# Decode through two attention and GEGLU layers on one core: layer norm in two products, a transpose inside PSUM, the gate's second half in two pieces, and one more V head kept

## The chip, the cores and the metric

The kernel runs on 1 core of a Trainium2 chip, as one launch. The metric is the device time of that core in microseconds (us). The kernel before was timed in three runs: 293.29, 294.82 and 295.31 us, median 294.82. A separate execution was recorded by the hardware profiler; it took 291.89 us, and its instructions span 290.1 us.

## What is computed

Two layers, each attention followed by a feed-forward block, with **the same weights and the same K/V cache in both layers**. There are 4 batches of one token each, width 512, 32 query heads over 8 K/V heads of 128, a cache of 4096 positions, and a feed-forward width of 1792. All inputs are bf16.

```python
def _A_ref(x, k_cache, v_cache, wq, wo):
    q = (x @ wq) ...                                   # 32 heads of 128
    scores = jnp.einsum("bhqd,bhkd->bhqk", q, k) * (Dh ** -0.5)
    p = _softmax(scores, axis=-1)
    o = jnp.einsum("bhqk,bhkd->bhqd", p, v)
    return o ... @ wo

def _B_ref(x, w_gate, w_up, w_down):
    return (_gelu(x @ w_gate) * (x @ w_up)) @ w_down

x = A_x
x = x + _A_ref(_layernorm(x), A_k_cache, A_v_cache, A_wq, A_wo)
x = x + _B_ref(_layernorm(x), B_w_gate, B_w_up, B_w_down)
x = x + _A_ref(_layernorm(x), A_k_cache, A_v_cache, A_wq, A_wo)
x = x + _B_ref(_layernorm(x), B_w_gate, B_w_up, B_w_down)
```

A K or V head of one batch is 4096 x 128 bf16, which is 1 MB. All K and V of the four batches together are 64 MB, the weights are some 13.5 MB.

## The kernel before

**Order of the work.** A small planner (class `Plan`) is given every step with its engine, an estimated duration and its dependencies. It lays the steps out in a list, the one with the longest remaining path first, shifted by the table `LEAD`. The list is then emitted step by step, so each engine runs its own steps strictly in the planned order and waits in place when a step isn't ready. The planner's durations decide order only; they aren't times of the chip. Each step's name appears below in quotes.

**Batches and layers.** The batches go one after the other. Inside batch b the first layer (L = 0) runs whole: scores of all 8 heads ("sc", in two halves z of four heads, each in two parts m), softmax ("mx", "bi", "ex", "pt", "pw", "pc", with the sums "su" and "rc"), values head by head ("val", in two halves m of 16 products), scaling by the softmax sum ("os"), output projection ("op", with the half sums "yo" and "ys"), layer norm, and feed-forward ("up", "ft", "ga" and so on to "dn"). Then follow a layer norm, the query projection of the second layer ("qm", "qe", "qt", "qs", "qp", "qx") and the second layer's scores. The second layer's values of batch b are computed while batch b+1 loads and runs its first layer. The second layer's projection and feed-forward are done once, for all four batches, at the very end.

**Loads.** All large loads are issued by SyncE (SP) in one fixed order, and each load is spread over all 16 DMA engines. K and V go through 12 slots of 1 MB each (`SLOTS`, tile KV). A load waits, on SP, until the last reader of its slot's old contents is done; everything behind it on SP waits too. K of batch b is loaded once and serves both layers. V is loaded once per layer, except for the heads in `HELD[b]`, which keep their slot from the first layer to the second. `HELD` is `((), (7,), (7,), (7,))`: in batch 0 no head is kept. The loads in `HALVES` come as two loads of 512 KB (`ld_part`, L357), the others whole (`ld_head`, L351). After the down-projection weights come the K heads of batch 1: as long as free slots last they are issued early, the others wait for the second layer's first scores of batch 0, step ("sc", 0, 1, 0, 1), which frees four slots.

**Steps named in the prediction.** K heads are transposed on VectorE (DVE) in place, two steps per head ("tn", L366). The layer norm squares x ("lnq", L500), sums x and x² in one fp32 product into R_ps[1] ("lnm", L506), takes both sums with one reduction (L512), subtracts the mean (L513) and computes the variance ("lnv", L521 and L522). The query projection of half z is a product into R_ps[z] (L538), copied to SBUF as bf16 by ScalarE (ACT) ("qe", L551), transposed by DVE (L556), spread with a mask ("qs", L595), replicated by a small product ("qp", L605) and expanded into the scores' weights ("qx", L392). In the feed-forward both products come out with tokens on partitions; "ft" (L662) transposes one of them from PSUM to SBUF on DVE; "ga" (L678 to L681) and an exponential on ACT (L688) make the gelu's argument; L697 and L699 multiply by the norm's factor and by the other half; L705 to L707 finish the gelu and write the bf16 product; L715 is the down projection; L646 and L647 transpose its result and add it to x.

At the end of the kernel the values of batch 3's second layer run in the order of heads 0, 1 to 3, 7, 4 and 5, 6. The projection of all but head 6 goes into R_ps[0] (L613); its two halves are copied by ACT (L632) and summed into R_ps[1] by products (L639), and head 6's own products (L623) are added there. Spare products of the identity (L1004) fill waits on TensorE (PE).

Of the kernel before, what the change touches and what calls it, by code (L numbers as in the profile page):

```python
# [11 lines left out]
ACT = mybir.ActivationFunctionType  # L12
# [9 lines left out]
HELD = ((), (7,), (7,), (7,))  # L22
HALVES = {(b, 1, j) for b in range(3) for j in range(8)} | {(3, 1, 6)}
# [7 lines left out]
DMA_FETCH = 1.5  # L31
DMA_LEAD = 4.0

PATIENCE = (0.5, 1.5, 0.7)
LEAD = {"tn1": -3, "val0": 1, "sc10": -2, "chain": 2, "sc11": -6, "sm00": 1, "os0": -6, "op": -2, "sm01": 11, "sm10": 10, "qx1": 4, "other": 5, "sc00": 2, "sm11": 8, "os1": -4, "tn0": -2, "sc01": 1}
EARLY = {("pt", 1): 60.0, ("su", 1): 60.0}
WINDOW = 3.413
WARM = 0.45
FILL = 0.7
SPIN = 0.22  # L40
STREAM = {"sc": 0.85, "qm": 0.85, "up": 0.75, "up2": 0.75, "kt": 0.21, "pw": 0.16, "qp": 0.11, "qn": 0.05,
          "su": 0.02, "lnm": 0.03, "xt": 0.1, "ys": 0.2, "dn": 0.38, "dn2": 0.38}


def stage(n):
# [13 lines left out]
    if n[0] in ("lnq", "lnm", "lnc", "lnv", "lnr", "up", "ft", "ga", "gb", "gy", "gc", "zz", "dn", "da", "qm", "qe",  # L59
                "qt", "qn", "qc", "qk"):  # L60
        return "chain"
# [3 lines left out]
class Plan:  # L65
# [149 lines left out]
    def warm(self, places):  # L215
# [3 lines left out]
        for n, _ in self.order:  # L219
# [16 lines left out]
            past.append((z, last, 0.72 * d if kind == "val" else d - 0.15 if kind in ("op", "op2") else STREAM.get(kind, 0.0)))  # L236
# [4 lines left out]
def kernel(  # L241
# [22 lines left out]
    FT = F // 4  # L264
    scale = float(Dh) ** -0.5
# [237 lines left out]
    def ln_mm(bs, nb):  # L503
        def emit():
            st = R_ps[1][:, 0:2 * CD * nb].rearrange("p (s k b) -> p s k b", s=2, k=CD)
            nc.tensor.matmul(st, lhsT=ones_mean, rhs=XS[:, :, :, bs], start=True, stop=True)  # L506
        return emit

    def ln_mid(bs, nb):
        def emit():  # L510
            st = R_ps[1][:, 0:2 * CD * nb].rearrange("p (s k b) -> p s b k", s=2, k=CD)
            nc.vector.tensor_reduce(out=mu[:, :, 0:nb], in_=st, axis=AX.X, op=ALU.add)  # L512
# [5 lines left out]
    def ln_var(nb):  # L518
        def emit():
            t = lt[:, 0:nb]  # L520
# [12 lines left out]
    def qmm(z, bs, nb):  # L533
# [7 lines left out]
        return emit  # L541

# [46 lines left out]
    def qsplit(z, b):  # L589
        def emit():  # L590
            if b:
# [17 lines left out]
    def proj(src, nb, heads, first, last):  # L609
        def emit():  # L610
            for j in heads:
                for i in range(4):
                    nc.tensor.matmul(R_ps[0][32 * i:32 * i + nb, :], lhsT=src[:, 4 * j + i, 0:nb],  # L613
# [4 lines left out]
    def proj_last(src, nb, heads, last):  # L618
# [433 lines left out]
```

## Time and profile before

| quantity | value |
| --- | --- |
| median of three runs | 294.82 us (293.29 to 295.31) |
| profiled execution | 291.89 us, span of its instructions 290.1 us |
| HBM read | 111.42 MB, 384 GB/s over the span |
| PE busy | 236.3 us (81%), 67.7 of it the spare products of L1004 |
| DVE busy | 133.5 us (46%) |
| ACT busy | 74.5 us (26%) |
| granted TensorE clock | 0.998 of full speed |

Busy time of an engine says little here: PE fills its waits with products that compute nothing. The rows of use are those of the DMA engines, the chain of waits (which follows the work that ended last back to what released it), and the timeline. In timelines, a row gives the start in us from the span's start, the duration, the engine, the line, the operation and how many instructions were merged; in brackets stands the idle time before it and what ended it.

### The profile page before, as it was taken

Reading aid. Unit: us, or ns where it says so; the run is one execution under the profiler, and the core shown is the slowest. Engines: PE = TensorE matmul, PEld = TensorE weight load, DVE = VectorE, ACT = ScalarE, POOL = GpSimd, SP = SyncE. Lnnn points to the kernel's source line nnn. Section 1 sums busy time; section 2 is a strip of 40 time slices with the busy share of each in tenths; the row PEclk is TensorE's granted clock in tenths of the full one; section 3 lists DMA queues with packets and bytes.
Section 4 is the critical chain, followed back from the end, with each engine's and each line's share of the span. In section 5 each row is a group of like instructions: output and inputs, shape, how many; then the busy total and the mean of one; then the engine's idle time right before and its main releaser. Section 6 shows DMA issues by size and latency. Waiting matters only on the chain.

```text
span 290.1 us, 9733 instructions
## 1 busy us (share of the span) xinstructions
PE 236.3 (81%) x4419; PEld 138.3 (48%) x4419; DVE 133.5 (46%) x380; ACT 74.5 (26%) x167; POOL 0.7 (0%) x6
## 2 busy tenths in 40 slices
PE   4988887878687888798888698879977889897794
PEld 1433454443233565455434465554445655565552
DVE  4149911002289942052389721343998213444034
ACT  1020751001023852101224731000338321113010
POOL 0000000000000000000000000000000000000000
PEclk9999999999999999999999999999999999999999
DMA  7999999999999999999999999999999999999910
GB/s 312 412 421 419 376 405 416 414 371 426 415 407 395 419 421 417 402 407 406 393 417 416 425 416 411 405 407 390 413 422 416 408 387 403 396 382 420 411 47 1
DMA packets 21657, 112.04 MB, mean 386 GB/s; under 512 B 2032, under 2 KB 6128, under 8 KB 12272
## 3 DMA queue, kind: packets, MB, share of 16 engines
q1 hardware_dynamic: 21568, 111.42, 95.3%
q8 instruction: 34, 0.56, 0.8%
q14 instruction: 7, 0.06, 0.0%
q10 hardware_dynamic: 48, 0.01, 0.0%
HBM read 111.42 MB, written 0.00 MB: 384 GB/s over the span
## 4 chain that ended last, share of the span: by engine, by line
DMA 62%; PE 16%; SPq 11%; DVE 7%; issue 2%; ACT 1%; DVEq 0%
DMA KV<-in_A_v_cache_dram 43%; DMA KV<-in_A_k_cache_dram 8%; SPq L351 7%; PE O_ps L485 7%; DMA wd_sb<-in_B_w_down_dram 6%; DMA wq_sb<-in_A_v_cache_dram 5%; SPq L741 3%; PE S_ps L415 3%; DVE KV L366 2%; PE R_ps L715 1%; PE R_ps L538 1%; DVE PA L662 1%; PE S_ps L1004 1%; PE R_ps L655 1%; DVE sm L421 1%
## 5 line engine op out<-in xcount | busy, mean ns | idle before, releaser
L485 PE MATMUL O_ps<-PA,KV 128*128 128x56 bf16 x1920 | 66.3, 188 | 20.8 <-DMA KV<-in_A_v_cache_dram 17.3
L485 PEld LDWEIGHTS <-KV 128*128 128x128 bf16 x1920 | 57.6, 97 | 40.8 <-DMA KV<-in_A_v_cache_dram 32.4
L1004 PE MATMUL S_ps<-iden_b 128*128 128x512 bf16 x226 | 67.7, 401 | 3.6 <-DVE iden_b L321 3.6
L366 DVE STREAM_TRANSPOSE KV<-KV 128x1024 int32<-128x1024 int32 x48 | 56.5, 1214 | 0.6 <-DMA KV<-in_A_k_cache_dram 0.4
L379 ACT ACTIVATE KV<-R_ps 128x512 bf16<-128x512 f32 x64 | 34.9, 595 | 28.0 <-PE R_ps L373 27.9
L415 PE MATMUL S_ps<-KV,PA 128*32 128x512 bf16 x384 | 35.3, 394 | 2.1 <-DVE KV L366 1.3
L1004 PEld LDWEIGHTS <-iden_b 128*128 128x128 bf16 x227 | 21.9, 107 | 27.6 <-issue 11.7
L373 PE MATMUL R_ps<-iden_b,KV 128*128 128x128 bf16 x256 | 22.1, 219 | 6.3 <-ACT KV L379 3.1
L421 DVE TENSOR_REDUCE sm<-S_ps 128x1 f32<-128x512 f32 x16 | 10.8, 677 | 27.4 <-PE S_ps L415 27.4
L373 PEld LDWEIGHTS <-KV 128*128 128x128 bf16 x256 | 15.8, 97 | 14.8 <-issue 10.2
L415 PEld LDWEIGHTS <-PA 128*32 128x32 bf16 x384 | 11.4, 94 | 13.2 <-issue 4.4
L493 DVE TENSOR_TENSOR OT<-O_ps,XS 128x4 bf16<-128x4 f32 (+1 forms) x12 | 2.0, 164 | 32.9 <-PE O_ps L485 32.9
L415 PE MATMUL S_ps<-KV,QN 128*32 128x512 bf16 x128 | 16.8, 381 | 0.2 <-ACT KV L379 0.2
L438 ACT ACTIVATE PA<-S_ps,sm 128x512 bf16<-128x512 f32 x16 | 11.7, 732 | 20.4 <-DVE sm L432 17.6
L632 ACT ACTIVATE PA<-R_ps 128x256 f32<-128x256 f32 x10 | 3.8, 384 | 46.2 <-PE R_ps L613 41.1
L529 ACT ACTIVATE sm<-sm 128x1 f32<-128x1 f32 (+1 forms) x10 | 2.0, 203 | 52.6 <-DVE sm L522 52.6
L493 DVE TENSOR_TENSOR OT<-O_ps,rdk 128x16 bf16<-128x16 f32 (+3 forms) x18 | 3.1, 170 | 26.7 <-PE O_ps L485 26.7
L463 ACT ACTIVATE PA<-T_ps 128x512 bf16<-128x512 f32 x16 | 9.6, 597 | 13.0 <-PE T_ps L455 11.8
L556 DVE STREAM_TRANSPOSE PA<-PA 128x256 int32<-128x256 int32 x10 | 4.4, 437 | 14.9 <-ACT PA L551 14.2
L613 PE MATMUL R_ps<-wo_sb,OT 128*1 128x512 bf16 (+1 forms) x124 | 8.7, 378 | 2.6 <-DMA wo_sb<-in_A_wo_dram 1.4
L646 DVE STREAM_TRANSPOSE PA<-R_ps 128x128 f32<-128x128 f32 x9 | 2.9, 317 | 16.5 <-PE R_ps L623 10.2
L447 DVE STREAM_TRANSPOSE PA<-PA 128x256 int32<-128x256 int32 x16 | 7.0, 434 | 7.5 <-ACT PA L438 7.5
(92 smaller groups left out, 173.9 us busy)
## 6 DMA issues: line engine op xcount, KB each, us to landing
KV<-in_A_v_cache_dram SPq DMA_DIRECT2D x34, 1024.0 KB, 15.0
KV<-in_A_k_cache_dram SPq DMA_DIRECT2D x32, 1024.0 KB, 13.5
KV<-in_A_v_cache_dram SPq DMA_DIRECT2D x46, 512.0 KB, 7.0
wq_sb<-in_A_wq_dram SPq DMA_DIRECT2D x1, 4096.0 KB, 12.2
wo_sb<-in_A_wo_dram SPq DMA_DIRECT2D x2, 2048.0 KB, 19.5
wq_sb<-in_A_v_cache_dram SPq DMA_DIRECT2D x4, 1024.0 KB
wg_sb<-in_B_w_gate_dram SPq DMA_DIRECT2D x1, 1792.0 KB
wu_sb<-in_B_w_up_dram SPq DMA_DIRECT2D x1, 1792.0 KB
```

The costliest lines, as they stand in the source:

```text
L351: nc.sync.dma_start(out=where[name], in_=src.rearrange("(p c) d -> p (c d)", p=P))
L366: nc.vector.transpose(out=w, in_=w)
L373: nc.tensor.matmul(R_ps[k % 2][:, P * u:P * u + P], lhsT=where[name][:, at:at + P], rhs=iden_b[:], start=True, stop=True)
L379: nc.scalar.activation(out=where[name][:, 512 * k:512 * k + 512], in_=R_ps[k % 2][:], func=ACT.Copy)
L415: nc.tensor.matmul(S_ps[z][32 * t:32 * t + 32], lhsT=w, rhs=k, start=(m == 0 and x == 0), stop=(m == 1 and x == 3))
L421: nc.vector.tensor_reduce(out=cms[:, z:z + 1], in_=S_ps[z][:].rearrange("p c r -> p (c r)"), axis=AX.X, op=ALU.max)
L438: nc.scalar.activation(out=PW[L][z].rearrange("p (a r e) -> p a r e", a=8, e=2), in_=S_ps[z][:].rearrange("p (a e) r -> p a r e", e=2), fu ...
L463: nc.scalar.activation(out=PW[L][z], in_=T_ps[z][:].rearrange("p t x -> p (t x)"), func=ACT.Copy)
L485: nc.tensor.matmul(Ov[L][:, j], lhsT=vw[:, c, :], rhs=w[:, c // 2, :, c % 2].unsqueeze(1).broadcast_to([P, WIDE, 4]), start=(m == 0 and c ...
L613: nc.tensor.matmul(R_ps[0][32 * i:32 * i + nb, :], lhsT=src[:, 4 * j + i, 0:nb], rhs=wo_sb[:, 4 * j + i, :], start=(first and j == heads[0 ...
L741: return lambda pick: nc.sync.dma_start(out=dst, in_=src.rearrange(pat, q=P))
L1004: nc.tensor.matmul(sinks[place].rearrange("p (a n) -> p a n", a=4), lhsT=iden_b[:], rhs=every, start=True, stop=True)
```

## The change

The change has five parts.

1. `HELD[0]` becomes `(7,)`: V head 7 of batch 0 stays in its slot until the second layer has used it, and its second load (two loads of 512 KB) goes away. One slot fewer is free while batch 0's first layer ends; the fourth K head of batch 1, ("k", 1, 3), therefore no longer finds a slot early and waits for ("sc", 0, 1, 0, 1), and ("v", 1, 0, 3) waits for the second layer's values of head 7.
2. The layer norm's sums come from two products in two banks. The mean's product doesn't wait for the square; the mean's reduction, the subtraction and the product that follows don't wait for the square's sum.
3. In the second layer, half z = 0 of the query projection writes its columns in another order, so that DVE can transpose the fp32 result in place in PSUM, and the spread reads PSUM. ACT's copy of that half goes away.
4. In the feed-forward, gelu's gate (all but the last multiplication) is finished ahead of the other product's transpose. That transpose and the last multiplication are cut in two pieces, 8 and 6 of 14 chunks, and so are the down projection and its weights' loads (before: 7 and 7).
5. At the end, heads 4, 5 and 6 are scaled apart, the half sums go ahead of the projections of heads 5 and 6, and both of these go directly into R_ps[1].

The planner's constants and its table `LEAD` were set anew, so the order on the engines shifts in other places too. In batch 0, DVE's built order now has the first K transpose of batch 1 between the spread and the expansion of the second layer's first half (before: ahead of the spread's transpose, in the wait for ACT). In batch 3, both "up" products now stand ahead of the second half of head 6's values of batch 2.

```diff
-HELD = ((), (7,), (7,), (7,))
-HALVES = {(b, 1, j) for b in range(3) for j in range(8)} | {(3, 1, 6)}
+HELD = ((7,), (7,), (7,), (7,))
+HALVES = {(b, 1, j) for b in range(3) for j in range(7)} | {(3, 1, 6)}
...
-DMA_FETCH = 1.5
+DMA_FETCH = 0.8
...
-PATIENCE = (0.5, 1.5, 0.7)
+PATIENCE = (0.5, 1.5, 0.1)
...
+    CUT = (0, 8, CF)
...
+    def ln_place(s, nb):
+        return O_ps[0][:, 512 - CD * nb:] if s else R_ps[1][:, 0:CD * nb]
+
+    def ln_mm(s, bs, nb):
+        def emit():
+            st = ln_place(s, nb).rearrange("p (k b) -> p k b", k=CD)
+            nc.tensor.matmul(st, lhsT=ones_mean, rhs=XS[:, s, :, bs], start=True, stop=True)
+        return emit
...
+    def qmm_apart(bs):
+        def emit():
+            for c in range(CD):
+                w = wq_sb[:, c, :].rearrange("q (z g h j k e) -> q z g h j e k", z=2, g=2, h=8, j=2, e=2)
+                for jg in range(4):
+                    nc.tensor.matmul(R_ps[0][32 * jg:32 * jg + 1, :].rearrange("p (h e k) -> p h e k", h=8, e=2),
+                                     lhsT=xn[:, c, bs], rhs=w[:, 0, jg % 2, :, jg // 2],
+                                     start=(c == 0), stop=(c == CD - 1))
+        return emit
+
+    def qturn_apart():
+        nc.vector.transpose(out=R_ps[0][:], in_=R_ps[0][:])
...
-            g = [[7], [6, 5, 4], [3, 2, 1, 0]] if b < B - 1 else [[0], [1, 2, 3], [7], [4, 5], [6]]
+            g = [[7], [6, 5, 4], [3, 2, 1, 0]] if b < B - 1 else [[0], [1, 2, 3], [7], [4], [5], [6]]
...
-        a = add(("lnq", tag), "DVE", 0.17, [after], ln_sq(bs, nb))
-        a = add(("lnm", tag), "PE", 0.4, [a], ln_mm(bs, nb), ins=4)
-        a = add(("lnc", tag), "DVE", 0.37, [a], ln_mid(bs, nb))
-        v = add(("lnv", tag), "DVE", 0.33, [a], ln_var(nb))
+        s = add(("lnq", tag), "DVE", 0.17, [after], ln_sq(bs, nb))
+        m = add(("lnm", tag), "PE", 0.35, [after], ln_mm(0, bs, nb), ins=4)
+        a = add(("lnc", tag), "DVE", 0.3, [m], ln_mid(bs, nb))
+        s = add(("lns", tag), "PE", 0.35, [s, m], ln_mm(1, bs, nb), ins=4)
+        v = add(("lnv", tag), "DVE", 0.45, [s, a], ln_var(nb))
...
+    def ffn(tag, a, bs, nb, y, clear=None):
+        one = nb == 1
+        g = [None, None]
+        for z, w in ((0, wg_sb), (1, wu_sb)):
+            g[z] = add(("up", tag, z), "PE", 0.93, [a, g[0], "wu" if z else "wg"], up(z, w, bs, nb), ins=32)
+        t0 = add(("ft", tag, 0), "DVE", 0.65, [g[0]], ffturn(0))
+        a = add(("ga", tag), "DVE", 0.59 if one else 0.72, [t0, ("lnr", ("f", tag))], gelu_a(nb, y))
+        e = add(("gb", tag), "ACT", 0.22 if one else 0.25, [a], gelu_b(nb))
+        if not one:
+            a = add(("gz", tag), "DVE", 0.28, [a], gelu_z(nb, y))
+        e = add(("gd", tag), "DVE", 0.72 if one else 0.95, [e, a], gelu_d(nb, y))
+        t1, h, n = a, None, None
+        for k in range(2):
+            t1 = add(("ft", tag, 1 + k), "DVE", (0.44, 0.36)[k], [g[1], t1], ffturn(1, k))
+            h = add(("gh", tag, k), "DVE", 0.18, [t1, e, h], gelu_h(nb, k))
+            if k and clear:
+                add(("zz", tag), "DVE", 0.07, [h], clear)
+            n = add(("dn", tag, k), "PE", (0.55, 0.42)[k], [h, n, ("wd", k)], down(nb, k), ins=8 * (CUT[k + 1] - CUT[k]))
+        return n
...
+    p, y = parts(B - 1, 1), rs
+    a = outproj(("op", "last"), p, len(p) - 2, 1, al, B, [dense_end], [])
```

More of the change, by code (lines that the diff above doesn't have):

```diff
@@ L590, in emit @@
         def emit():
-            if b:
+            if b == "apart":
+                q = R_ps[0][:].rearrange("p (h e x) -> p x e h", h=8, e=2)[:, 0]
+            elif b:
                 q = qc[:, z, b - 1].rearrange("p (h e) -> p e h", e=2)
@@ L607, in qrep, with proj @@
         return emit
-    def proj(src, nb, heads, first, last):
+    def proj(src, cols, nb, heads, first, last):
         def emit():
@@ L712, in emit @@
             h = ff(nb)[3]
-            for c in range(7 * k, 7 * k + 7):
+            for c in range(*CUT[k:k + 2]):
                 for t in range(4):
@@ L911 @@
                     for m in range(2):
[L912 removed]
+                        add(("tn", b, j, m), "DVE", 1.22, [("k", b, j)], turn(("k", b, j), m))
             s = None
```

145 lines of the change are left out of this document (65 added, 80 removed).

## The prediction

> **What bounds the kernel now.** I read the page first: the rates, the queues, the chain of waits; then the DMA share in short windows; then the chain and the timeline at the places that the change touches.
>
> ```profile
> GB/s 312 412 421 419 376 405 416 414 371 426 415 407 395 419 421 417 402 407 406 393 417 416 425 416 411 405 407 390 413 422 416 408 387 403 396 382 420 411 47 1
> ...
> q1 hardware_dynamic: 21568, 111.42, 95.3%
> ...
> DMA 62%; PE 16%; SPq 11%; DVE 7%; issue 2%; ACT 1%; DVEq 0%
> ...
> KV<-in_A_v_cache_dram SPq DMA_DIRECT2D x46, 512.0 KB, 7.0
> ```
>
> Over 38 of 40 slices the rate hardly leaves 370 to 426 GB/s, and 62% of the chain is loads landing. The windows (us; busy time and count by engine; granted clock; DMA share; GB/s) show where the loads pause and where they end:
>
> ```profile
> 86.50:87.00 0.50, 0.50 (x18) 0.37 (x15) 0.50 (x2) 0.18 (x1) 0.00 (x0) 1.00 0.68 279
> 87.00:87.50 0.50, 0.50 (x4) 0.21 (x3) 0.44 (x2) 0.00 (x0) 0.00 (x0) 1.00 0.79 295
> 87.50:88.00 0.50, 0.44 (x3) 0.09 (x1) 0.46 (x4) 0.00 (x0) 0.00 (x0) 1.00 0.72 279
> ...
> 94.00:274.00 180.00, 150.08 (x3245) 96.31 (x3238) 86.12 (x243) 53.49 (x119) 0.00 (x0) 1.00 1.01 408
> ...
> 276.00:278.00 2.00, 1.95 (x53) 1.21 (x50) 0.18 (x1) 0.03 (x1) 0.00 (x0) 1.00 0.28 104
> 278.00:280.00 2.00, 2.00 (x57) 1.31 (x54) 0.30 (x2) 0.74 (x2) 0.00 (x0) 1.00 0.00 0
> ```
>
> From 94 to 274 us the DMA engines are full (share 1.01). The pause that concerns this change is at 86.5 to 88.0: 0.32, 0.21 and 0.28 of half a microsecond each, 0.40 us in the mean. After 276 only stragglers run. So the span is load time up to about 278, then a chain of 12 us. Time is won by moving fewer bytes, by not pausing, or in that chain; DVE, ACT and PE work elsewhere is cover.
>
> **Head 7 kept: the bytes.** One MB goes: 1.049 MB at the 408 GB/s above is 2.57 us.
>
> **Head 7 kept: the pause.** The slot it keeps was the fourth K head's early place. That load then stands on SP until the second layer's first scores of batch 0 are done, and the 72 MB of later KV loads stand behind it. The SP rows before (issue from the timeline, and each one's time to landing):
>
> ```profile
> 65.98 0.33 SPq L351 DMA_DIRECT2D KV<-in_A_k_cache_dram  x1
> ...
> 86.42 3.08 SPq L351 DMA_DIRECT2D KV<-in_A_k_cache_dram  x4
> ...
> 259.83 0.33 SPq L357 DMA_DIRECT2D KV<-in_A_v_cache_dram  x1
> ...
> KV<-in_A_k_cache_dram SPq DMA_DIRECT2D x1, 1024.0 KB, 23.3
> ...
> KV<-in_A_v_cache_dram SPq DMA_DIRECT2D x1, 512.0 KB, 18.6
> ```
>
> The fourth K head was issued at 65.98 and landed 23.3 later, at 89.3; the next was issued at 86.42, when the scores were done. Most DMA engines had run dry by 86.5 to 87, the slowest only at 89.3: the engines are apart by 2 us and more. At the end likewise: the last load lands at 259.83 + 18.6 = 278.4 with the mean share already at 0.28. Without the fourth head queued, every engine runs dry 2.5 us earlier (1 MB), and what ends the pause is the path to those scores. That path before, from the chain of waits and, last two rows, the timeline:
>
> ```profile
> 78.90 0.59 PE R_ps L715 x28
> ...
> 80.07 0.18 DVE XS L500
> ...
> 80.29 0.40 PE R_ps L506 x2
> ...
> 81.16 1.04 PE R_ps L538 x16
> ...
> 82.22 0.61 ACT PA L551
> ...
> 82.85 0.46 DVE PA L556
> ...
> 83.33 0.27 DVE qs L595
> ...
> 83.65 0.23 PE T_ps L605 x4
> ...
> 83.91 0.43 DVE PA L392
> ...
> 81.38 1.25 DVE L366 STREAM_TRANSPOSE KV<-KV 128x1024 int32<-128x1024 int32 x1
> ...
> 84.39 2.02 PE L415 MATMUL S_ps<-KV,PA 128*32 128x512 bf16 x32 [0.21 <-DVE PA L392]
> ```
>
> It starts when the last down-projection weights land, which nothing ahead of them changes. Step by step:
> - Down projection: 24 products behind those weights instead of 28, 0.59 x 4/28 = 0.08 less.
> - Square: the mean's product no longer waits for it, 80.29 - 80.07 = 0.22 less.
> - First half's copy and turn: 82.22 to 83.31, 1.09, become one in-place turn of 128x512 fp32 in PSUM. The trace has no such turn. Two from PSUM to SBUF are near:
>
> ```profile
> L662 DVE STREAM_TRANSPOSE PA<-R_ps 128x448 f32<-128x448 f32 x10 | 6.5, 648 | 7.2 <-PE R_ps L655 7.1
> ...
> L646 DVE STREAM_TRANSPOSE PA<-R_ps 128x128 f32<-128x128 f32 x9 | 2.9, 317 | 16.5 <-PE R_ps L623 10.2 <-PE R_ps L715 6.3
> ```
>
>   The slope is (648 - 317)/320 = 1.03 ns per element, the fixed part 0.185 us; 512 elements take 0.715. Bounds: 0.65 (the 448 row) and 1.1 (no gain against the copy). I take 0.72: 0.37 less.
> - K transpose: it now stands between the spread and the expansion on DVE. Before, it ran from 81.38 in ACT's shadow, and the expansion waited only for the small product: 83.60 to 83.91, 0.31. After, the expansion waits for 1.25 + 0.02: 0.96 more.
>
> Sum: -0.08 - 0.22 - 0.37 + 0.96 = +0.3. The scores end, and the issue comes, at 86.7 instead of 86.4. New data of an issue come some 1.3 us later: an estimate from the issue at 86.42 and shares that are back at full only at 88. So they flow from 88.0, and the fourth K head lands at about 90.8 on all engines, as they start together.
>
> What the pause costs has two accounts. By the mean engine it grows by up to 2.5 + 0.3 = 2.8 us, 0.2 more than the MB saved. By the slowest engine, which sets each landing: before, the fifth K head could land at 89.3 + 2.5 = 91.8; after, at 90.8 + 2.5 = 93.3, 1.5 later, against 2.57 saved: 1.1 won. Bounds: a loss of 0.2 and a gain of 1.3 (the path 0.2 shorter). I take 0.6, between the two but nearer to the slowest engine's account, since a step waits for a whole load. [...]
>
> **Batches 1 to 3.** The norm, the in-PSUM turn and the early gate shorten chains that lie beside full DMA queues: nothing, while each load is issued early enough. A half load takes 7.0 us from issue to landing (median above); an empty queue would need about 1.3 + 1.25 + 0.4 = 3.0. In batch 3, both up products now stand ahead of a value step that frees a half slot; they take about 1.7 us together (0.96 for one below), and 4.0 of margin cover that. In the first layer norm the next product waits for its weights anyway.
>
> **The end.** Chain of waits before, from the last value products on:
>
> ```profile
> 278.80 0.54 PE O_ps L485 x16
> ...
> 279.34 0.39 PE R_ps L639 x4
> 279.73 0.29 PE R_ps L623 x16
> ...
> 280.12 0.33 DVE PA L646
> ...
> 280.47 0.18 DVE XS L647
> ...
> 281.81 0.96 PE R_ps L655 x16
> ...
> 284.26 0.56 DVE PA L662
> ...
> 285.85 0.23 DVE PA L707
> ...
> 286.12 0.98 PE R_ps L715 x56
> ...
> 287.12 0.29 DVE PA L732
> ```
>
> - Heads 5 and 6: last landing 278.4 to the turn at 280.12 is 1.7. After: 0.06 hop, 0.54 values, 0.29 for head 5 (over head 6's scaling), 0.29 for head 6, 0.1 of hops: 1.3. 0.4 less.
> - Norm: the square goes from the path, 0.2 less.
> - Feed-forward: one more turn (0.185 fixed), one more multiplication (0.2, as L707), and about 0.12 of waiting for the exponential, which the whole turn at 284.26 used to cover; against that only 24 of 56 down products stay behind the last multiplication: 0.98 - 0.44 = 0.54 less. Sum 0; bounds ±0.2. [...]
>
> End: -0.6, from -0.9 to -0.2.
>
> **Sum.** -0.6 for loads, -0.6 for the end: -1.2 on the profiled execution's 291.89 us (span 290.1 to 288.9). On the median of 294.82 that is 293.6. The three runs differ by 2 us, so 1% (2.9 us) is about what can be told from no change.
>
> **Rivals.**
> 1. *The MB pays in full*: the pause doesn't grow, because the path gets shorter than I think (K transpose hidden, engines apart enough): -2.57 - 0.6 = -3.2, 291.6. For it: the engines' 2 us of spread. Against it: K transpose on the path. Chance 0.14, faster by just over 1%.
> 2. *The loads run dry behind the value steps*: the half-slot ring of batches 1 to 3 gets late where the feed-forward steps stand ahead of value products on PE. It decides once such a step delays an issue by more than the 4.0 us of margin; at 1.5 us of pause in each of three batches, 4.5 - 1.2 = +3.3: 298.1. Against it: share 1.01 over 180 us, and the batch 3 shift is 1.7. Chance 0.10, slower.
> 3. *Kept head, no gain*: the mean engine's account and a slow PSUM turn (+0.4), with an end that gains only 0.2: 0.2 + 0.4 - 0.2 = +0.4, 295.2. The change saves the MB but not its time. Chance 0.16, within 1%.
>
> The forecast has 0.60. Faster 0.15, within 1% 0.75, slower 0.10 (rounded, runs' spread taken in). At their ends, the forecast's terms give -1.3 - 0.9 = -2.2 (292.6) and +0.2 - 0.2 = 0 (294.8). Taking in rival 3, most of rival 1 and 1 us of the runs' spread, the range is 291.3 to 296.2.
>
> **What would show it.** HBM read 110.37 MB. A pause between about 84.5 and 88 with a mean share that misses some 3 us. The scores' issue at 86.4 to 87, with a 1.25 us transpose between L595's and L392's successors. The in-place turn at 0.65 to 0.8 us. Loads ending near 277.8. From last landing to the addback's turn 1.3; from its end to the up products 0.95. Wrong if the share from 94 to 274 falls under 0.98 (rival 2), if the pause stays under 1 us (rival 1), or if the down products end more than 0.2 us later after the up products than before.

## The result, and the profile after

The changed kernel took 294.33 us (median of 20 runs, 293.17 to 296.31). The kernel before, run 20 times on the same chip, took 293.00 us (291.62 to 295.31; the three runs shown first are among these). The ratio is 1.0051, with a 95% interval of 1.0029 to 1.0072: slower by about 1.5 us, where 1.2 us less was forecast. The profiled execution took 295.07 us, its span is 293.1 us against 290.1. The two profiled executions lie on opposite sides of their medians (0.7 above, and 291.89 us before, 1.1 below), so the traces differ by about twice what the medians do.

The 3.0 us of span divide at two points that the rows below give. The last load lands at 261.47 + 17.9 = 279.4 (before 278.4): 1.0 later. From there to the turn that adds the projection to x it is 282.93 - 279.4 = 3.5 (before 1.7): 1.8 more. From that turn to the end it is 10.2 (before 10.0): 0.2 more. A second trace of the changed kernel (after_again, below) lands at 279.2 and has 3.6 and 10.2 us behind that.

Of the page of the changed kernel: the queues (packets, MB, share), the bytes, and the chain's shares.

```profile
q1 hardware_dynamic: 21280, 110.37, 93.4%
q8 instruction: 34, 0.56, 0.8%
...
HBM read 110.37 MB, written 0.00 MB: 377 GB/s over the span
...
DMA 54%; PE 22%; DVE 12%; SPq 4%; issue 3%; ACT 3%; DVEq 0%; ACTq 0%
```

The MB is gone (111.42 before), yet the mean rate fell from 384 to 377 GB/s. Loads have 54% of the chain (62% before), PE 22% (16%).

**The pause.** Window 84 to 89 us, first of the kernel before, then of the changed one:

```profile
84.00:89.00 5.00, 4.01 (x59) 1.81 (x58) 4.57 (x11) 1.35 (x4) 0.00 (x0) 1.00 0.92 369
```

```profile
84.00:89.00 5.00, 4.45 (x80) 2.43 (x82) 4.38 (x13) 0.18 (x1) 0.00 (x0) 1.00 0.41 161
```

The share fell from 0.92 to 0.41: the mean pause grew from 5 x 0.08 = 0.40 us to 5 x 0.59 = 2.95. The rate fell by 208 GB/s, which over 5 us is 1.04 MB: about the MB that was saved. The path to the scores that end the pause, from the chain of the changed kernel:

```profile
79.23 0.53 PE R_ps L746 x24
...
82.37 0.74 DVE R_ps L563
...
83.37 1.01 DVE KV L367
84.38 0.06 issue
84.44 0.40 DVE PA L393
...
84.88 2.05 PE S_ps L416 x30
```

The in-place turn (L563) takes 0.74. The K transpose (L367) holds the expansion (L393) for 1.01, as the built order said. From the first down product to the end of the scores it is 86.93 - 79.23 = 7.70; before, 78.90 to the issue at 86.42, 7.52.

**TensorE waits for its own instructions.** The timeline of PE, the rows whose idle time the profile ends with "issue" (the engine waited for nothing else that it shows), and then the windows between them:

```profile
256.71 0.60 PE L546 MATMUL R_ps<-wq_sb,xn 128*1 128x512 bf16 x7 [2.40 <-issue]
...
262.90 0.94 PE L486 MATMUL O_ps<-PA,KV 128*128 128x56 bf16 x29 [0.91 <-issue]
...
269.10 0.21 PE L486 MATMUL O_ps<-PA,wq_sb 128*128 128x56 bf16 x2 [0.33 <-issue]
...
275.02 0.27 PE L486 MATMUL O_ps<-PA,KV 128*128 128x56 bf16 x4 [1.36 <-issue]
```

```profile
256.70:262.89 6.19, 5.29 (x128) 3.74 (x128) 2.12 (x7) 1.07 (x4) 0.00 (x0) 1.00 1.03 422
262.89:269.09 6.20, 5.78 (x128) 4.17 (x128) 2.63 (x12) 2.33 (x5) 0.00 (x0) 1.00 1.01 419
269.09:275.01 5.92, 4.17 (x128) 3.69 (x128) 0.84 (x4) 0.60 (x1) 0.00 (x0) 1.00 1.01 413
```

Between two such waits stand 128 products and 128 weight loads each time, 256 instructions, and 5.9 to 6.2 us, with full DMA queues. The page's row for q8, an instruction queue, fits this: 0.56 MB in 34 packets of 16 KB, and 34 x 256 = 8704 against TensorE's 2 x 4456 = 8912 instructions. In the trace, four of these packets begin at 254.3, 260.4, 266.5 and 272.7 and take 1.0 to 1.1 us, and each of the four waits ends 1.2 to 1.5 us after the end of one. Below I call one such packet a refill. The kernel before has these waits too, at other places and mostly smaller:

```profile
250.03 0.56 PE L715 MATMUL R_ps<-wd_sb,PA 128*1 128x128 bf16 x26 [0.66 <-issue]
...
255.96 0.19 PE L485 MATMUL O_ps<-PA,KV 128*128 128x56 bf16 x1 [0.46 <-issue]
...
262.15 0.29 PE L485 MATMUL O_ps<-PA,KV 128*128 128x56 bf16 x5 [1.21 <-issue]
...
274.55 0.45 PE L485 MATMUL O_ps<-PA,KV 128*128 128x56 bf16 x11 [0.32 <-issue]
```

**What the last one does.** Windows of the changed kernel around it (the third last column is the granted clock), then the last load's row on SP's timeline and its time to landing, and the chain from there:

```profile
274.00:275.00 1.00, 0.00 (x0) 0.00 (x0) 0.00 (x0) 0.00 (x0) 0.00 (x0) 1.00 1.02 418
275.00:276.00 1.00, 0.98 (x20) 0.70 (x20) 0.17 (x1) 0.00 (x0) 0.00 (x0) 0.82 0.93 377
276.00:279.00 3.00, 3.00 (x45) 1.46 (x42) 0.17 (x1) 0.00 (x0) 0.00 (x0) 0.50 0.33 130
279.00:280.00 1.00, 1.00 (x33) 0.68 (x26) 0.00 (x0) 0.38 (x1) 0.00 (x0) 0.97 0.00 0
```

```profile
261.47 0.34 SPq L358 DMA_DIRECT2D KV<-in_A_v_cache_dram  x1
```

```profile
KV<-in_A_v_cache_dram SPq DMA_DIRECT2D x1, 512.0 KB, 17.9
```

```profile
281.62 0.54 PE O_ps L486 x16
282.15 0.69 PE R_ps L647 x32
...
282.93 0.33 DVE PA L670
...
284.38 0.96 PE R_ps L679 x16
...
288.77 1.05 PE R_ps L746 x56
289.82 0.02 issue
289.84 0.29 DVE PA L765
```

TensorE stood still from 273.7 to 275.0 in the middle of head 7's values; then the granted clock was 0.50 until about 279. In 276 to 279 it ran 45 products; the same stretch of a later run without the wait has 68. So the values of the last head, whose data were there at 279.4, began only at 281.62, 2.2 later. The profile names no wait there: PE was simply behind.

**The loads of batch 3.** Of the 1.0 us by which the last load lands later, some 0.4 stand before this stage (the last down-projection weights of batch 0's first layer land 0.3 later, and the load issued at 240.4 lands at 249.5, against 249.15 before). Another loss lies between 250 and 253 us. First the kernel before: the value step that frees a half slot, and the load that waited for it; then the changed kernel, where that step stands behind both up products (48 products in one row); then 250 to 253 us, before and after:

```profile
244.37 0.59 PE L485 MATMUL O_ps<-PA,KV 128*128 128x56 bf16 x16
244.99 0.33 SPq L357 DMA_DIRECT2D KV<-in_A_v_cache_dram  x1
```

```profile
246.65 1.47 PE L486 MATMUL O_ps<-PA,KV 128*128 128x56 bf16 x48
247.28 0.33 SPq L358 DMA_DIRECT2D KV<-in_A_v_cache_dram  x1
```

```profile
250.00:253.00 3.00, 2.89 (x77) 1.89 (x76) 1.30 (x8) 0.41 (x2) 0.00 (x0) 1.00 1.03 397
```

```profile
250.00:253.00 3.00, 2.92 (x73) 1.96 (x70) 1.58 (x7) 0.00 (x0) 0.00 (x0) 1.00 0.98 287
```

The load comes 2.3 us later, and 250 to 253 us move 287 GB/s in place of 397, although the share is still 0.98: the share counts the time that packets take, and here they took longer. The loads' queue has 236 packets at a share of 98.3% there, 0.983 x 48 / 236 = 0.20 us each in the mean on 16 engines; before, 325 at 102.6%, 0.15 us each. At the rate of before, the bytes of these 3 us would have taken 0.8 us less. Against the kernel before most of it comes back at once, since that has a slow stretch of its own at 253 to 258 (349 GB/s, 408 in the changed kernel). Over 246 to 258 us the changed kernel moves 371 GB/s, the kernel before 378 and kept_alone 399: 0.2 and 0.8 us of 12. The rest of the 1.0 us isn't traced. No refill wait over 0.25 us stands between 197 and 254 us, so no refill wait explains the loss. In all 11 traces of the changed kernel and its variants but three_mended, this load comes 3.2 us behind the one ahead of it, and 246 to 258 us move 338 to 371 GB/s; in the traces of before, kept_alone and new_plan it comes 1.1 to 1.3 us behind, and they move 378 to 408.

### The profile page after: what moved, and what is told of

The parts are those of the page before. It is cut to its first block, busy times and chain, and to the rows that moved or that the text cites. A ratio compares the mean times of both kernels' runs of the same rounds, so it can differ in the third digit from the quotient of the medians.

```text
span 293.1 us, 9818 instructions
## 1 busy us (share of the span) xinstructions
PE 240.6 (82%) x4456; PEld 144.5 (49%) x4456; DVE 136.3 (47%) x401; ACT 72.1 (25%) x163; POOL 0.7 (0%) x6
## 3 DMA queue, kind: packets, MB, share of 16 engines
q1 hardware_dynamic: 21280, 110.37, 93.4%
HBM read 110.37 MB, written 0.00 MB: 377 GB/s over the span
## 4 chain that ended last, share of the span: by engine, by line
DMA 54%; PE 22%; DVE 12%; SPq 4%; issue 3%; ACT 3%; DVEq 0%; ACTq 0%
DMA KV<-in_A_v_cache_dram 37%; PE O_ps L486 7%; DMA wd_sb<-in_B_w_down_dram 6%; DVE KV L367 5%; DMA wq_sb<-in_A_v_cache_dram 5%; PE S_ps L1043 4%; DMA KV<-in_A_k_cache_dram 4%; PE S_ps L416 3%; SPq L774 3%; DMA PA<-in_A_x_dram 2%; ACT KV L380 1%; PE R_ps L557 1%; PE R_ps L746 1%; DVE sm L422 1%; PE R_ps L637 1%
## 5 line engine op out<-in xcount | busy, mean ns | idle before, releaser
L486 PEld LDWEIGHTS <-KV 128*128 128x128 bf16 x1920 | 58.4, 97 | 38.6 <-DMA KV<-in_A_v_cache_dram 26.3
L367 DVE STREAM_TRANSPOSE KV<-KV 128x1024 int32<-128x1024 int32 x48 | 56.5, 1212 | 0.7 <-DMA KV<-in_A_k_cache_dram 0.5
L374 PE MATMUL R_ps<-iden_b,KV 128*128 128x128 bf16 x256 | 22.9, 223 | 8.0 <-DMA KV<-in_A_k_cache_dram 4.6
L374 PEld LDWEIGHTS <-KV 128*128 128x128 bf16 x256 | 16.5, 99 | 15.6 <-issue 9.1
L416 PEld LDWEIGHTS <-PA 128*32 128x32 bf16 x384 | 12.2, 95 | 11.6 <-issue 4.3
L494 DVE TENSOR_TENSOR OT<-O_ps,rdk 128x4 bf16<-128x4 f32 (+2 forms) x19 | 3.2, 170 | 30.1 <-PE O_ps L486 30.0
L416 PE MATMUL S_ps<-KV,QN 128*32 128x512 bf16 x128 | 15.9, 380 | 0.2 <-ACT KV L380 0.2
L573 ACT ACTIVATE PA<-R_ps 128x512 bf16<-128x512 f32 x4 | 2.4, 597 | 37.7 <-PE R_ps L546 37.7
L688 DVE STREAM_TRANSPOSE PA<-R_ps 128x448 f32<-128x448 f32 (+2 forms) x15 | 7.3, 490 | 6.8 <-PE R_ps L679 6.8
```

What stands on the lines that cost most here:

```text
L367: nc.vector.transpose(out=w, in_=w)
L374: nc.tensor.matmul(R_ps[k % 2][:, P * u:P * u + P], lhsT=where[name][:, at:at + P], rhs=iden_b[:], start=True, stop=True)
L416: nc.tensor.matmul(S_ps[z][32 * t:32 * t + 32], lhsT=w, rhs=k, start=(m == 0 and x == 0), stop=(m == 1 and x == 3))
L486: nc.tensor.matmul(Ov[L][:, j], lhsT=vw[:, c, :], rhs=w[:, c // 2, :, c % 2].unsqueeze(1).broadcast_to([P, WIDE, 4]), start=(m == 0 and c ...
L688: nc.vector.transpose(out=PD[:, 32 * c0:32 * c1].rearrange("p (c x) -> p c x", x=32), in_=R_ps[z][:, 0:FT].rearrange("p (r c) -> p c r", c ...
```

## The experiments

All ratios are to the kernel before, run in turn on the same chip, with 95% intervals. Two theories were tested. **A**: the kept head's MB is eaten by the pause, which follows the path to the freed slots. **B**: the rest is lost to refills of TensorE's instructions that fall badly, and to the clock behind them. The loads of batch 3 were not among the theories; one run, three_mended, bears on them.

### kept_alone

```diff
-HELD = ((), (7,), (7,), (7,))
-HALVES = {(b, 1, j) for b in range(3) for j in range(8)} | {(3, 1, 6)}
+HELD = ((7,), (7,), (7,), (7,))
+HALVES = {(b, 1, j) for b in range(3) for j in range(7)} | {(3, 1, 6)}
```

> The kernel before with head 7 of batch 0 kept, and nothing else of the change. Theory A (the kept head's 1.05 MB is eaten by the pause before batch 1's second-layer-dependent loads, because the fourth K head has lost its early slot): the mean DMA pause between 84 and 89 us grows from 0.4 us to 2.2 to 3.0, the last load lands within 0.7 us of the kernel before, the time is within 0.3% of it. Rival (the MB pays in full): pause under 1 us and 2.5 us faster (ratio 0.991). Rival (the kept head is what makes the changed kernel slower): ratio 1.004 or more.

Ratio 1.0015 (0.9996 to 1.0035). Its window, and its last load:

```profile
84.00:89.00 5.00, 4.04 (x62) 1.84 (x58) 4.62 (x10) 1.43 (x4) 0.00 (x0) 1.00 0.43 146
```

```profile
259.83 1.03 SPq L357 DMA_DIRECT2D KV<-in_A_v_cache_dram  x1
```

```profile
KV<-in_A_v_cache_dram SPq DMA_DIRECT2D x1, 512.0 KB, 18.3
```

The pause is 2.85 us, 2.45 more than before, and the last load lands at 278.1 against 278.4. The MB buys 0.3 us of loads and no time that can be measured. Theory A holds for the loads: the load issued at 240.1 lands at 249.2 in both kernels. The end adds something of its own here: a refill wait of 0.95 us stands at 274.3 (0.32 before), and from landing to turn it is 2.2 us in place of 1.7, with the granted clock at 1.00.

### all_but_kept

The changed kernel with the two lines above turned back.

> The changed kernel without the kept head: V head 7 of batch 0 is loaded twice again, all other parts stay. Theory A: the pause falls back to about 0.4 us, 111.42 MB are read, and the time is that of the changed kernel within 0.3% (saved pause and added MB cancel). Theory B (the loss sits at the end, where TensorE waited 1.36 us for its instructions inside head 7's values and then ran at a granted clock of 0.5): the time depends on where that wait falls; with a wait of over 1 us after 270 us the ratio to the kernel before is 1.004 or more, without one it is 0.999 or less, since the path after the last landing is otherwise about 0.5 us shorter than before. Rival (the kept head costs 1.5 us): ratio 1.000 or less, whatever the end looks like.

Ratio 1.0116 (1.0079 to 1.0154): a miss. The pause did fall back (share 0.92 in 84 to 89) and the MB came back, but it is slower than the changed kernel by 0.65%, which neither theory forecast: no refill wait of over 1 us stands behind 270 us. The planner made another order, and TensorE had a refill wait of 1.96 us at 257.7, followed by a granted clock of 0.5 for some 3 us; the last load lands at 280.9. What the kept head is worth inside the changed kernel can't be told from this run.

### shift_60, shift_60_again, plus_60, after_again

In the first two, the 30 spare products ahead of the very first query projection are left out; plus_60 adds 30 tiny ones instead; after_again is the changed kernel once more. The order of all other steps is the same.

```diff
-            if name in idle:
+            if name in idle and name != ("qm", "i", 0):
                 spin(*idle[name])
```

```diff
                 spin(*idle[name])
+            if name == ("qm", "i", 0):
+                for _ in range(30):
+                    nc.tensor.matmul(S_ps[0][:].rearrange("p c r -> p (c r)")[:, 0:4], lhsT=iden_b[:],
+                                     rhs=iden_b[:, 0:4], start=True, stop=True)
```

> The changed kernel without the 30 spare products ahead of the very first query projection, 60 TensorE instructions fewer; order and all else are the same. Only the places at which TensorE's stream of instructions is refilled (every 256 instructions) move, by 60 instructions against the work. Theory B: the waits of 2.40 us at 254 and 1.36 us at 274 us move or change size; if none over 0.8 us is left after 265 us, the granted clock stays above 0.9 to the end, the time from the last landing to the first turn behind the projection falls from 3.54 to about 1.7 us, and the time falls by 1 to 2 us (ratio to the kernel before 0.998 to 1.001). If such a wait is still there, the time stays. Rival (the end's new order costs the 1.9 us): last landing to turn stays above 3 us and the ratio at 1.004 or more, although the wait has moved.

> The changed kernel once more, beside the same kernel with its refills shifted, to see what repeats. Theory B (the wait of 1.36 us inside head 7's values comes from where the refill falls, so it repeats): a refill wait of 0.7 to 1.8 us again inside head 7's values, at 273 to 275 us; ratio 1.003 to 1.007. Rival (chance of one execution): no wait over 0.5 us there.

> The changed kernel without the 30 spare products at the start, once more. Theory B: again no refill wait over 0.5 us between 268 and 280 us, the last landing to the turn within 1.4 to 1.7 us unless the granted clock falls for another reason, and the median at least 0.5 us under that of the changed kernel in this call. Rival (the first difference was noise): the medians lie within 0.4 us, or a wait of over 0.7 us stands late again.

> The changed kernel with 30 tiny products more (60 TensorE instructions) ahead of the first projection: the refills fall 60 instructions earlier against the work, the other way than without the 30 spares. Theory B: the refill that fell inside head 7's values now falls in the values of heads 2 and 3, TensorE gets there earlier and waits 1 us or more, or a later one meets the last values; the time depends on what is left behind it, ratio 1.003 to 1.010. Rival (the place of the refills doesn't matter): within 0.1% of the changed kernel's ratio in this call.

| kernel | instructions against the changed kernel | ratio | 95% |
| --- | --- | --- | --- |
| shift_60 (first series) | -60 | 1.0027 | 1.0001 to 1.0054 |
| shift_60_again | -60 | 1.0008 | 0.9979 to 1.0036 |
| after_again | 0 | 1.0059 | 1.0029 to 1.0088 |
| plus_60 | +60 | 1.0111 | 1.0061 to 1.0160 |

The last three ran in one series. 120 instructions that compute nothing, at the start of the kernel, move the time by 1%. The spares do hold the first query projection (it begins at 12.9 us without them, at 17.3 with them), but nothing of that is left later: the first products behind the down-projection weights of batch 0 begin at 79.2 to 79.4 us in all five traces. The two traces of the changed kernel agree with each other: after_again has its refill waits at the same places (2.13 us at 256.7, 0.91 at 262.8, 1.49 at 275.0), and the clock at 0.5 behind the last. Without the 60, neither trace has a refill wait over 0.5 us after 263 us. So after_again and shift_60_again came out as expected; in the first series the end did, and the ratio (1.0027) stayed above the 0.998 to 1.001 expected. The end of shift_60_again: the same windows, the last load, and the chain.

```profile
276.00:279.00 3.00, 3.00 (x68) 1.78 (x65) 0.24 (x2) 0.38 (x1) 0.00 (x0) 1.00 0.48 188
```

```profile
262.67 0.33 SPq L358 DMA_DIRECT2D KV<-in_A_v_cache_dram  x1
```

```profile
KV<-in_A_v_cache_dram SPq DMA_DIRECT2D x1, 512.0 KB, 17.2
```

```profile
280.14 0.54 PE O_ps L486 x16
280.68 0.68 PE R_ps L647 x32
...
281.45 0.33 DVE PA L670
```

Landing at 279.9, turn at 281.45: 1.6 (1.45 in shift_60), against 3.5 in the changed kernel. The last load itself lands no earlier than there (279.3 and 279.9, against 279.4): what the shift brings back is the end.

In plus_60 the ratio is just above the 1.003 to 1.010 expected, and the place that I had named is wrong. No refill wait fell into the late values; the bad ones came earlier, and cost loads. Its row at 256 us and the windows behind:

```profile
256.22 0.62 PE L486 MATMUL O_ps<-PA,KV 128*128 128x56 bf16 x17 [2.32 <-issue]
```

```profile
256.00:258.00 2.00, 1.78 (x41) 1.03 (x44) 0.42 (x1) 0.00 (x0) 0.00 (x0) 0.84 0.89 330
258.00:260.00 2.00, 2.00 (x24) 0.80 (x20) 0.00 (x0) 0.60 (x1) 0.00 (x0) 0.50 0.85 229
```

Values finish late, so their slots come free late, and the DMA share dips below full; the last load landed at 282.3, 2.9 later than in the changed kernel (this execution took 298.02 us, 2.5 over its median). PE then waits for a load, the granted clock is 0.50 from 275 to 281 us (0.61 in 274 to 276, 0.50 in 276 to 279, 0.62 in 279 to 282), and from landing to turn it is 3.8 us:

```profile
274.95 1.67 PE L486 MATMUL O_ps<-PA,wq_sb 128*128 128x56 bf16 x32 [2.79 <-DMA wq_sb<-in_A_v_cache_dram]
```

So the refills cost in two ways here: PE falls behind at the end (3.5 us from landing to turn in the changed kernel), or loads are issued late (the last one lands 2.9 us later in plus_60). The half clock followed a wait for a load here (2.79 us), as it followed one for a refill in the changed kernel (1.36 us).

### before_60

The kernel before with the same 30 tiny products.

> The kernel before with 30 tiny products (4 columns each, about 1 us together) added ahead of the very first query projection: 60 TensorE instructions more, nothing else. Theory B (where the refills of TensorE's instructions fall sets part of the end): the refill that costs 0.32 us at 274.5 us in the kernel before now meets the values 60 instructions earlier; the wait there grows to 0.8 to 1.9 us, the last landing to the turn behind the projection from 1.68 to 2.2 us or more (3.5 or more if the granted clock falls to 0.5 behind the wait, as it did behind waits of 1.36, 1.65 and 1.71 us), and the time rises by 0.5 to 2 us: ratio 1.002 to 1.007. Rival (refills are noise, the changed kernel's own parts cost the time): ratio within 0.998 to 1.0015, last landing to turn at 1.6 to 1.9 us.

Ratio 1.0010 (0.9979 to 1.0042): theory B's numbers were not met, and both of the rival's were: the ratio, and 1.8 us from landing to turn. The trace has refill waits of 1.18 us at 261.6 and 0.88 at 267.8 and none over 0.3 us later, but that execution took 298.67 us against a median of 293.98, so its places prove little. Sixty instructions more are not bad in themselves. That it depends on what the refills meet fits all these runs, but this one doesn't show it.

### turn_behind, both_mended, three_mended, path_clean

These shorten the path to the freed slots in the changed kernel. The first moves the K transpose; the second adds the 60 instructions fewer; the other two also move the small products of the other batches' queries.

```diff
+    at = [n for n, _ in order]
+    step = order.pop(at.index(("tn", 1, 0, 0)))
+    order.insert([n for n, _ in order].index(("qx", 0, 1, 0)) + 1, step)
```

> The changed kernel with the first K transpose of batch 1 moved on VectorE from ahead of the expansion of the second layer's first half to right behind it. Theory A: the path to the scores that free the four slots gets about 0.95 us shorter, the loads' issue comes 0.9 us earlier after the down-projection weights' landing (6.8 in place of 7.7 us), the mean pause falls from 3.0 to about 2.1 us, and the last load lands 0.9 us earlier; the time falls by 0.9 us (ratio 0.003 lower than the changed kernel's 1.005). Rival (the transpose is hidden, or the scores then wait for it as long): issue and pause stay within 0.2 us, time the same.

> The changed kernel with two edits: the first K transpose of batch 1 right behind the expansion, and without the 30 spare products ahead of the first query projection (60 TensorE instructions fewer). Theories A and B together: the issue comes 6.8 us after the down-projection weights' landing, the pause is about 2.2 us, no refill wait over 0.8 us is left after 265 us, the granted clock stays above 0.9 there, and the two gains add: ratio 0.998 to 1.001. Rival (the two gains were one, or execution noise): ratio 1.002 to 1.004, as each alone gave.

> The changed kernel with four steps moved and 60 TensorE instructions fewer: the first K transpose of batch 1 right behind the expansion; the 16 small products of the other batches' queries and their copy behind the scores that free the four slots; the second half of head 6's values of batch 2 ahead of both up products of batch 3; no 30 spare products ahead of the first projection. Theories A and B: the scores start when the expansion is done (84.0 to 84.1 us, in place of 84.46 with the transpose alone moved), the issue comes at 86.0 to 86.2 us, the pause is 1.8 to 2.1 us, no load gap over 0.3 us stands at 247 to 258 us, and the ratio is 0.995 to 0.999. Rival (the pause doesn't follow the path, or another wait ends it): pause 2.3 us or more, ratio 0.999 to 1.003.

three_mended moves ("qn", 0), ("qc", 0) and ("val", 2, 1, 6, 1) in the same way, before the spare products are placed; path_clean moves the first two after that, and drops the spare products of ("qn", 0) and of the scores:

```diff
+    behind(("tn", 1, 0, 0), ("qx", 0, 1, 0))
+    behind(("qc", 0), ("sc", 0, 1, 0, 1))
+    behind(("qn", 0), ("sc", 0, 1, 0, 1))
+    for n in (("qm", "i", 0), ("sc", 0, 1, 0, 0), ("qn", 0)):
+        idle.pop(n, None)
```

> The changed kernel with the path to the four slots cleared: the first K transpose of batch 1 behind the expansion, the 16 small products of the other batches' queries, their copy and the two spare products behind the scores that free the slots; and without the 30 spare products at the start. With the transpose alone moved, the scores started at 84.46, 0.45 us after the expansion was done, since spare products and those 16 stood ahead of them on TensorE. Theory A: scores start at 84.0 to 84.1 us, the issue comes at 86.0 to 86.2 us, the mean pause is 0.4 us shorter than with the transpose alone moved (1.9 to 2.2 us), and the ratio is 0.995 to 0.9995. Rival (the issue is held by another wait): issue at 86.4 or later.

| kernel | scores start | mean pause | ratio | 95% |
| --- | --- | --- | --- | --- |
| changed kernel | 84.88 | 2.95 | 1.0051 | 1.0029 to 1.0072 |
| turn_behind | 84.46 | 2.35 | 1.0024 | 1.0006 to 1.0041 |
| both_mended | 84.5 | 2.50 | 0.9993 | 0.9964 to 1.0022 |
| three_mended | 84.45 | 2.45 | 1.0024 | 0.9990 to 1.0057 |
| path_clean | 84.08 | 2.15 | 0.9986 | 0.9957 to 1.0014 |

turn_behind won 0.4 of the 0.95 us: the next thing was late, PE's own queue. Its last load lands 0.7 us earlier than the changed kernel's, and its end differs too: it has the same stream of PE instructions, but the refill wait in head 7's values is 0.77 us in place of 1.36, the granted clock stays at 1.00, and from landing to turn it is 2.0 us. So its gain is not the pause's alone. both_mended's ratio came out as expected, though its granted clock fell to 0.50 for a while behind two waits for loads, at 269 to 272 us. three_mended won nothing more, and its numbers are those of its rival. PE's timeline of three_mended, behind the product that replicates the query, then that product and the scores of path_clean:

```profile
83.48 1.04 PE L1043 MATMUL S_ps<-iden_b 128*128 128x512 bf16 x4
84.45 2.06 PE L416 MATMUL S_ps<-KV,PA 128*32 128x512 bf16 x32
```

```profile
83.34 0.21 PE L629 MATMUL T_ps<-qs,fold_b 128*32 128x64 bf16 x4 [0.23 <-DVE qs L619]
84.08 2.07 PE L416 MATMUL S_ps<-KV,PA 128*32 128x512 bf16 x32 [0.53 <-DVE PA L393]
```

In three_mended the planner had filled the freed place with four spare products, and the scores stood behind them. With those gone, path_clean's scores start when the expansion is done, the issue comes at 86.1, and the pause is 0.8 us shorter than the changed kernel's. The pause follows the path. But the last load of path_clean lands at 279.3, as in the changed kernel: between 246 and 258 us it moves 354 GB/s (371 there, 378 before), which uses up what the shorter pause won. What its trace wins is the end, 1.4 us from landing to turn in place of 3.5. three_mended, which puts the value step back ahead of the up products, isn't a clean test of batch 3's loads: six spare products now stand ahead of that step, its load still comes 2.5 us behind the one ahead of it, and the rate is 355. The time of path_clean (292.61 us against 292.79) can't be told from that of the kernel before.

### old_plan, new_plan, end_as_before

Old_plan is the changed kernel with the planner's constants and table of before, new_plan the reverse. End_as_before undoes part 5 (groups `[4, 5], [6]`, and all but the last projection into R_ps[0]).

> The changed kernel, all five parts of it, but with the planner's constants and LEAD table of the kernel before. Theory D (the loss of the changed kernel is in the new order of the steps, not in the parts): the ratio falls from 1.005 to 1.000 or less; up products of batch 3 no longer stand ahead of a value step, so the loads at about 245 us are issued as early as in the kernel before. Rival (the parts themselves, or where TensorE's instruction refills fall): ratio 1.003 to 1.008, with the pause before batch 1's second-layer-dependent loads still at 2.2 to 3.1 us.

> The kernel before, none of the five parts, but with the planner's constants and LEAD table of the changed kernel. Theory D: slower by as much as the changed kernel or more, ratio 1.004 to 1.010. Rival (parts or refills): ratio within 0.998 to 1.003.

> The changed kernel with part 5 undone: heads 4 and 5 are scaled together, the half sums stand behind head 5's projection, only head 6's goes directly into the second bank. Theory B (the end lost to a late instruction refill on TensorE and the clock, not to its new order): where the trace has no refill wait over 0.8 us after 265 us, the last landing to the turn is 1.6 to 1.9 us, against 1.45 us in the changed kernel whose refills were shifted by 60 instructions; so part 5 is worth about -0.2 us, and the ratio is 1.003 to 1.007. Rival (the new order of the end costs 1 us or more): ratio 1.002 or less, and the last landing to the turn under 1.7 us even behind a late refill.

Old_plan: 1.0049 (1.0020 to 1.0078), with a refill wait of 1.71 us at 276.9, the clock at 0.5 behind it, and 4.3 us from the last landing to the turn. New_plan: 1.0093 (1.0058 to 1.0128). For old_plan the rival's ratio came out, for new_plan theory D's. The new constants aren't needed for the loss, since with the old ones the changed kernel is as slow; but by themselves they slow the kernel before by 0.9%, and not through the end's clock: that trace has no refill wait over 0.3 us after 263 us and a granted clock of 1.00, and its loads land 1.6 us later than before. Why is open. End_as_before: 1.0097 (1.0065 to 1.0130), above what was expected; here too a wait of 1.65 us in head 7's values, the clock at 0.5, and 4.7 us to the turn. Without such a wait, part 5's new order of the end took 1.4 to 1.6 us from landing to turn (shift_60, shift_60_again, path_clean), less than the 1.7 before, so part 5 isn't the cause. Its price can't be read from the ratio, because each plan puts the refills elsewhere.

## Why the prediction was wrong

**The step that failed, first: the value of the kept head.** Of its two accounts the prediction took 0.6, "nearer to the slowest engine's account, since a step waits for a whole load". kept_alone measured the mean engine's: 2.45 us of added pause against 2.57 saved, no time. The prediction's pause, its bytes and its path had been right: 110.37 MB, some 3 us missing between 84.5 and 88, the scores' end at 86.9 (86.7 forecast), the in-place turn 0.74 (0.72), the path 0.2 longer (0.3). Of its 1.3 us from an issue to new data: the share is 0.00 until 0.56 us behind the issue at 86.94, 0.38 and 0.31 in the two half microseconds after that, and 1.01 only then.

**Second, and larger: a term that was not in the sum.** The end's -0.6 took it that TensorE has its instructions and its full clock; in the traces the end is 2.0 us longer instead. The profile of before showed otherwise, in waits that end with "issue" and in the q8 row, and the prediction read neither; the planner in the source even has constants for such blocks of 256 (`BLOCK`, `FETCH`). The change has some 70 more PE instructions and another order, so other steps meet the refills. In the changed kernel one of them stops head 7's values for 1.4 us, and the half clock behind it takes the end's reserve: 3.5 in place of 1.7 us from landing to turn. Moved by 60 instructions, 1.45 to 1.6 us are left, and the time falls by 0.24% in one series and by 0.51% in the other.

**Third: "Batches 1 to 3: nothing".** The prediction named the step at fault, both up products ahead of a value step in batch 3, and had 4.0 us of margin cover it (its 3.0 us for an empty queue is my estimate, and no run shows its term of 0.4; the shortest half load of the kernel before, issued at 253.86, landed in 5.9 us). The load behind that step came 2.3 us later, and the margin did not cover it: 287 in place of 397 GB/s for 3 us, 0.8 us. That the order of that step causes it rests on the traces; no run changed it alone.

**The end by its terms**, where no refill disturbs it. Heads 5 and 6: 1.45 to 1.6 against 1.7, a gain of 0.1 to 0.2; 0.4 was forecast. Norm: from the turn to the up products 284.38 - 282.93 = 1.45 against 1.69, 0.24 less; 0.2 was forecast. Feed-forward: from the up products to the last down product 289.82 - 284.38 = 5.44 against 5.29, 0.15 more, within the forecast's 0 ± 0.2. Its two halves came out nearly as forecast: from the end of the last multiplication (286.08 before, 289.22 after) to the last down product it is 0.60 us in place of 1.02, 0.42 less (0.54 forecast), and the steps up to there take 0.57 more (0.5 forecast). The end as a whole gets no gain from this, since 0.3 us more stand behind the last down product; kept_alone, with the code of before, has these 0.3 too.

**Rivals.** Of the rivals, "kept head, no gain" came nearest, with its first half right. "The loads run dry behind the value steps" is what the traces show in a small size in batch 3, behind the feed-forward steps that it names; plus_60 shows loads running dry too, from refill waits. The sign chosen for it, a share under 0.98 from 94 to 274 us, could not have shown it: that share stayed at 1.01, and it was 0.98 even where the rate fell to 287 GB/s.

**Luck.** 294.33 us lies well inside the forecast's 291.3 to 296.2 because that range was built on 294.82, the median of three runs; 20 runs of the kernel before gave 293.00. Moved with it, the range is 289.5 to 294.4, and the measured time sits at its edge. The direction of the change was wrong.

How the 1.5 us divide is known only roughly. The shift by 60 brings back the end, 0.24 to 0.51%; the K transpose alone 0.27%; the two together (both_mended) 0.58%, path_clean 0.65% (1.9 us). The loads of batch 3 are brought back by none of them.

## What to carry to other kernels

The MB saved before a pause bought 0.3 us of loads in place of 2.57 (kept_alone), since the pause began that much earlier: ask what ends a pause, and shorten that path first. Read the waits that end with "issue" on the engine with the most instructions, and the instruction queue's row: here 256 instructions came every 5.9 to 6.2 us beside a DMA share of 1.01 to 1.03, TensorE waited up to 2.40 us for them, and 60 instructions left out at the start moved those waits against the work. Read the rate of the loads beside the DMA share, since here the share was 0.98 where the rate fell from 397 to 287 GB/s. Also compare two versions at several shifts of the instruction stream before an edit is credited with half a per cent: here 120 instructions that compute nothing moved the time by 1%.

## What the runs showed of the hardware

In the changed kernel a refill of 16 KB, for 256 TensorE instructions, arrived every 5.9 to 6.2 us while the DMA share was 1.01 to 1.03, and TensorE waited 2.40, 0.91, 0.33 and 1.36 us for four of them. Behind the last loads of the changed kernel the packets come 4.9 and 4.6 us apart (they begin at 272.7, 277.6 and 282.2).

Behind the wait of 1.36 us the granted clock was 0.82, 0.50 (for 3 us) and 0.97 in the windows above: 0.36 + 3.0 + 0.06 = 3.4 us at half speed. In after_again, all_but_kept and both_mended the half clock adds up to 3.4 us too, in plus_60 (274 to 282 us) to 1.56 + 3.00 + 2.28 = 6.84. In the changed kernel it followed a wait of 1.36 us, and in other runs 1.49 (after_again), 1.65 (end_as_before) and 1.71 (old_plan), while 2.40 us at 256.7 in the same execution as the first left the clock at 1.00, and so did 2.02 us at 262.6 in three_mended. What decides is not shown.
